# Two of every eight main P tiles moved into the remainder's transposing DMA, in the middle of the run too, with smaller rings for query, P and output

## The chip, the cores and the metric

The kernel runs on one core of one Trainium2 chip. The metric is the device time of one execution in microseconds (us). Three runs of the kernel before took 1221.61, 1224.74 and 1216.64 us, with a median of 1221.61.

## The reference

Two attention blocks, A and B, of the same shape are computed and their outputs set side by side. Each has its own x, K cache, V cache and weights, all bfloat16.

```python
B, Sq, D = 16, 144, 448
H, Sk, Dh = 16, 512, 256
q = (x @ wq).reshape(B, Sq, H, Dh).transpose(0, 2, 1, 3)
scores = einsum("bhqd,bhkd->bhqk", q, k_cache) * (Dh ** -0.5)
p = softmax(scores, axis=-1)
o = einsum("bhqk,bhkd->bhqd", p, v_cache)
out = o.transpose(0, 2, 1, 3).reshape(B, Sq, H * Dh) @ wo
```

The output is the concatenation of both blocks' `out` along the last axis.

## The kernel before

**Units and groups.** A unit is one (block, batch, head): 2 x 16 x 16 = 512 units. Eight units are a group (64 groups, called SG in the code); four are a half group (G). A head has 144 query rows, more than the 128 partitions. So the rows are split: 112 main rows ("A rows", QA) are treated unit by unit, and the 32 remaining rows ("B rows", QB) of four units are stacked into one 128-partition tile, so that a group has two B tiles.

**The work on a unit.** `t_q` (line 338) projects the query on TensorE into PSUM, and `t_evac_q` (lines 351, 355) brings it to `qt_sb`. `t_sa` (line 471) makes the scores of the A rows, `t_max` (482) takes the row maximum on VectorE, `t_exp` (493) the exponential on ScalarE into `pa_sb`, `t_recip` (503) and `t_norm` (511) normalise it, the latter on GpSimd (POOL in the profile). `t_ta` (524) transposes P on TensorE in four matmuls, and `t_evac_pta` (534) copies the result from PSUM to `pt_sb` on VectorE. `t_pv` (557) multiplies by V, `t_evac_ot` (572, 574) puts the result into the ring, and `t_op_piece` (595) does the output projection in pieces of two matmuls.

**The B rows.** `t_sb` (line 374) makes the scores of a whole group's B rows in 16 matmuls, followed by `t_max_b`, `t_exp_b` (397) and `t_norm_b` (415) into `pb_sb`. Their P reaches `pbt_sb` transposed in one of two ways. In the groups of `TB_SG` (0 to 7 and 28 to 37) TensorE does it (`t_tb`, line 437, four matmuls for each half group) and VectorE evacuates (447). In the other 46 groups one transposing DMA for the group does it (`t_ptb_dma`, line 425). `t_exp_b` writes its columns in the order that this DMA wants. From `pbt_sb`, which has one buffer, GpSimd copies each half group into `pt_sb` (`t_copy_ptb`, 457).

**Order.** All engines' programs are written out by one loop over slots `i`; a slot is the time of one unit's product with V (`t_pv(u)` at `i = u`). Group n's `t_sb` stands in slot 8n - lag, where the lag grows to 14 over the first groups (`LAGS`), and the eight `t_sa` of the group spread over the slots up to the next `t_sb`. TensorE runs its program strictly in this order. A B tile's copy to `pt_sb` stands in slots 8n - 1 and 8n + 1.

**Transfers.** All DMAs are issued by one queue, SyncE's (SP), in the order of `dma_plan`, which is sorted by planned slot; the `plan_*` functions hold each DMA's slot, its earliest slot and its deadline. Per group there are one K load of 2 MB (`t_load_k`, 306, a transposing DMA), two V loads of 1 MB (`t_load_v`, 316) and, outside `TB_SG`, the B rows' transposing DMA. Per four groups there is a load of x for two batches (`t_load_x`, 296 and 297, transposing too). K has two buffers (`NK`), so the K load of group n + 2 waits until the last `t_sa` of group n is done. From group 8 on the plan goes by pairs of groups:

```python
            plan_pb(t - 4, n)
            if n + 2 < NSG:
                plan_k(t - 3, n + 2)
            plan_pb(t + 2, n + 1)
            if n + 2 < NSG:
                plan_k(t + 2, n + 3)
            for j, at in enumerate((5, 5, 5, 8)):
                if 2 * n + 3 + j < NG:
                    plan_v(t + at, 2 * n + 3 + j)
```

The queue's order in a pair is thus: output stores and x (in every second pair), P of B rows, K of an even group, P of B rows, K of an odd group, four V. The weights of block B come in the middle of the run: `wq` in four blocks in slots 229 to 235 (lines 275, 277), `wo` around slots 277 and 293 (line 285).

Of the kernel before, what the change touches and what calls it, by code (L numbers as in the profile page):

```python
# [5 lines left out]
BF16 = mybir.dt.bfloat16  # L6
F32 = mybir.dt.float32
AF = mybir.ActivationFunctionType
ALU = mybir.AluOpType
# [3 lines left out]
PE, ACT, DVE, POOL, SP = "pe", "act", "dve", "pool", "sp"  # L13
# [109 lines left out]
def bass_concat_heads__mha_block_cached__gqa_block_cached__near_ridge_kernel(  # L123
# [20 lines left out]
    H, SK, DH = A_k_cache.shape[1], A_k_cache.shape[2], A_k_cache.shape[3]  # L144
    assert (SQ, D, SK, DH) == (144, 448, 512, 256), (SQ, D, SK, DH)
    assert H % 4 == 0
    QA, QB = 112, 32
    NU = Bn * H
    NT = NP * NU
    NG = NT // 4  # L150
    NSG = NT // 8
# [8 lines left out]
    NPC = NWO // OPP  # L160

    LT = 2
    LAGS = (7, 5, 6, 7, 8, 9, 10, 11, 12, 13, 14)
    RAMP = 8
    TB_SG = set(range(RAMP)) | set(range(NSG // 2 - 4, NSG // 2 + 6))
    NK, NV, NXG = 2, 5, 2
    WO_AT = ((12, 18, 26, 33), (277, 277, 293, 293))
    OP_FROM = (34, 34)
    N_WARM = (12, 16)
    XB = 2  # L170
    assert Bn % XB == 0
    NQT, NPA, NPB, NPT, NST, NSTB, NOST = 12, 14, 2, 8, 4, 2, 3
    NPBT = 1
    RS = 4
    RC = RS * 128
# [6 lines left out]
    with contextlib.ExitStack() as es:  # L182
        def sb(name, shape, dt):
            return es.enter_context(nc.sbuf_tensor(name, shape, dt))

        def ps(name, shape, dt):
            return es.enter_context(nc.psum_tensor(name, shape, dt))
# [6 lines left out]
        xt_sb = sb("xt_sb", [128, NXG, 4, XB * SQ], BF16)  # L194
        qt_sb = sb("qt_sb", [128, NQT, 2, SQ], BF16)
        pa_sb = sb("pa_sb", [128, NPA, SK], BF16)
        pb_sb = sb("pb_sb", [128, NPB, 2, SK], BF16)
        pt_sb = sb("pt_sb", [128, NPT, 4, SQ], BF16)
        pbt_sb = sb("pbt_sb", [128, NPBT, 2, 4, 128], BF16)
        ost_sb = sb("ost_sb", [128, NOST, D], BF16)  # L200
        ident = sb("ident", [128, 128], BF16)
        stat = sb("stat", [128, 3 * NST + 3 * NSTB + 2], F32)
        qp_ps = ps("qp_ps", [128, 512], F32)
        sa_ps = [ps("sa_ps%d" % i, [128, 512], F32) for i in range(2)]
# [6 lines left out]
        S = _Sched()  # L211
# [22 lines left out]
        NEG, RSUM, RINV = 0, NST, 2 * NST  # L234
# [3 lines left out]
        def t_ident():  # L238
            ones = pa_sb[:, 0, 0:128]

            def e1(g):
                return g.memset(ones, 1.0)
            S.add(POOL, e1, writes=[(("pa", 0), "ones")], name="ones")

            def e2(g):
                return g.affine_select(ident[:], ones, pattern=[[1, 128]], compare_op=ALU.is_equal,
                                       fill=0.0, base=0, channel_multiplier=-1)
            S.add(POOL, e2, reads=[(("pa", 0), "ones")], writes=[("ident", 0)], name="ident")

        def t_warm_zero():  # L250
            def e(v):
                return v.memset(pa_sb[:, 2:6, 0:128], 0.0)
            S.add(DVE, e, writes=[("warm", 0)], name="warmz")
# [166 lines left out]
        def t_ptb_dma(SG):  # L420
            psl = SG % NPB
            tsl = SG % NPBT

            def e(q):
                return q.dma_start_transpose(pbt_sb[:, tsl, :, :, :].rearrange("p g c q -> p (g c) q"),
                                             pb_sb[:, psl, :, :].rearrange("p g k -> p (g k)")).then_inc(
                    sems["pb%d" % tsl], 16)
            S.add(SP, e, reads=[(("pb", psl, g), (2 * SG + g, 1)) for g in range(2)],
                  writes=[(("pbt", tsl, g), SG) for g in range(2)], dma_sem="pb%d" % tsl, name="pb%d" % SG)

        def t_tb(G):
            psl = (G // 2) % NPB
# [19 lines left out]
        def t_copy_ptb(G):  # L452
            tsl = (G // 2) % NPBT
            s0 = (4 * G) % NPT

            def e(g):
                return g.tensor_copy(pt_sb[:, s0:s0 + 4, :, QA:SQ],
                                     pbt_sb[:, tsl, G % 2, :, :].rearrange("p c (j q) -> p j c q", j=4))
            S.add(POOL, e, reads=[(("pbt", tsl, G % 2), G // 2)], writes=[(("ptb", s0 + j), 4 * G + j) for j in range(4)],
                  name="cptb%d" % G)  # L460
# [16 lines left out]
        def t_max(U):  # L477
# [3 lines left out]
            def e(v):  # L481
# [2 lines left out]
            S.add(DVE, e, reads=[(("sap", bank), ("s", U))], writes=[(("neg", sl), U)], banks=["sa%d" % bank],  # L484
                  name="mx%d" % U)

        def t_exp(U):
            bank = U % 2
            sl = U % NST
            psl = U % NPA  # L490

            def e(a):
                return a.activation(pa_sb[0:QA, psl, :], sa_ps[bank][0:QA, :], AF.Exp,  # L493
                                    bias=stat[0:QA, NEG + sl:NEG + sl + 1], scale=1.0,
                                    accum_out=stat[0:QA, RSUM + sl:RSUM + sl + 1])
            S.add(ACT, e, reads=[(("sap", bank), ("s", U)), (("neg", sl), U)],
                  writes=[(("pa", psl), (U, 0)), (("rsum", sl), U)], banks=["sa%d" % bank], name="ex%d" % U)

        def t_recip(U):
            sl = U % NST  # L500
# [4 lines left out]

        def t_norm(U):
            sl = U % NST
            psl = U % NPA

            def e(g):  # L510
                return g.tensor_tensor(pa_sb[0:QA, psl, :], pa_sb[0:QA, psl, :],  # L511
                                       stat[0:QA, RINV + sl:RINV + sl + 1].to_broadcast([QA, SK]), op=ALU.mult)
            S.add(POOL, e, reads=[(("pa", psl), (U, 0)), (("rinv", sl), U)], writes=[(("pa", psl), (U, 1))],
                  name="nm%d" % U)

        def t_ta(U):
            psl = U % NPA
            bank = ta_bank[U]

            def e(t):  # L520
                src = pa_sb[0:QA, psl, :].rearrange("q (p c) -> q c p", c=4)
                ins = None
                for c in range(4):
                    ins = t.transpose(pta_ps[bank][:, c * 128:c * 128 + QA], src[:, c, :], ident[0:QA, 0:QA])  # L524
                return ins
            S.add(PE, e, reads=[(("pa", psl), (U, 1)), ("ident", 0)], writes=[(("sap", bank), ("t", U))],
                  banks=["sa%d" % bank], name="TA%d" % U)
# [101 lines left out]
        t_act_warm()  # L629
        t_wqzero()  # L630
        t_ident()
        t_warm_zero()
        ta_bank = {}
        lag = [LAGS[min(n, len(LAGS) - 1)] for n in range(NSG)]
        sb_slot = [8 * n - lag[n] for n in range(NSG)] + [8 * NSG - lag[-1]]
        sa_slot = [sb_slot[u // 8] + (u % 8) * (sb_slot[u // 8 + 1] - sb_slot[u // 8]) // 8 for u in range(NT)]
        q_slot = [sb_slot[0] - 1] * 8 + sa_slot[:NT - 8]
# [4 lines left out]
        tb_at = {}  # L642
        for n in TB_SG:
            t0 = 8 * n - 7
# [3 lines left out]
        s_min = sb_slot[0] - 4  # L648
        dma_plan = []

        def plan(at, lo, dl, fn, *args):
            assert lo <= at <= dl, (fn.__name__, args, lo, at, dl)
            dma_plan.append((at, len(dma_plan), fn, args))

        def plan_x(at, XG):
            n = XB * H
            plan(at, q_slot[(XG - 1) * n - 1] + 1 if XG >= NXG else s_min, q_slot[XG * n], t_load_x, XG)

        def plan_k(at, SG):
            plan(at, sa_slot[8 * (SG - NK) + 7] + 1 if SG >= NK else s_min, sb_slot[SG], t_load_k, SG)  # L660

        def plan_v(at, G):
            lo = 4 * (G - NV) + 3 + 1 if G >= NV else s_min
            plan(max(at, lo), lo, 4 * G, t_load_v, G)

        def plan_pb(at, SG):
            if SG not in TB_SG:
                plan(at, sb_slot[SG] + 5, 8 * SG - 1, t_ptb_dma, SG)
# [7 lines left out]
        for n in range(1, RAMP + 2):  # L676
            at = max(sb_slot[n] - 6, sa_slot[8 * (n - NK) + 7] + 1) if n >= NK else s_min + 2
# [10 lines left out]
        for n in range(RAMP, NSG, 2):  # L688
            t = 8 * n
            XG = (t + 32) // (XB * H)  # L690
            if (t + 32) % (XB * H) == 0 and XG < NXGT:
                plan_x(t - 4, XG)
            plan_pb(t - 4, n)
            if n + 2 < NSG:
                plan_k(t - 3, n + 2)
# [5 lines that stand above are left out]
                    plan_v(t + at, 2 * n + 3 + j)  # L701
        for hg in range(HG):
            lo = q_slot[NU - H + 4 * hg + 3] + 1
            plan((4.9, 4.9, 8, 11)[hg] + NU - 32, lo, q_slot[NU + 4 * hg], t_load_wq, 1, hg)
        dma_plan.sort(key=lambda t: t[:2])

        u_tail0 = NT - H
# [31 lines left out]
        i = s_min  # L739
        while True:  # L740
# [39 lines left out]
                t_copy_ptb((i + 1) // 4)  # L780
            if i % 8 == 1 and 0 <= i < NT:
                t_copy_ptb((i + 3) // 4)
            for u in sa_at.get(i - 1, ()):
                t_recip(u)
                t_norm(u)
            u = i + LT
            if 0 <= u < NT:
                ta_bank[u] = 1 - last_sa % 2 if sas else u % 2
                t_ta(u)
                t_evac_pta(u)  # L790
# [7 lines left out]
            u = i  # L798
            if 0 <= u < NT:
# [9 lines left out]
                if h == H - 1:  # L809
                    g_end = pr * RP + (b + 1) * SQ  # L810
                    lo = (pr * RP + b * SQ) // 128
# [80 lines left out]
```

## Time and profile before

| | |
|---|---|
| median of three runs | 1221.61 us |
| the profiled execution's own time | 1215.54 us |
| its span (first to last instruction) | 1213.8 us |
| mean granted TensorE clock | 0.992 |
| busy: TensorE matmuls / VectorE / ScalarE / GpSimd | 1171.0 / 743.7 / 748.6 / 727.9 us |
| chain that ended last | TensorE 80%, DMA 12%, VectorE 3%, GpSimd 2% |
| DMA | 679,424 packets, 304 MB on the queue of SP |
| the four P transposes of a unit on TensorE (line 524) | 2048 matmuls |
| their evacuation on VectorE (line 534) | 512 copies, 374 ns each |

The profile comes from one execution. Busy times of TensorE are unions of instructions whose ends are modelled, and matmuls overlap, so the time that a stage takes on TensorE is read from one stage's start to the next one's start. The landing of a DMA is the time of the last of its completions in the trace. "K of group n lands x us before `t_sb` of group n" is the slack of that load; where the slack is nearly nothing, TensorE waited for it.

### The profile page before, as it was taken

Reading aid. Unit: us, or ns where it says so; the run is one execution under the profiler, and the core shown is the slowest. Engines: PE = TensorE matmul, PEld = TensorE weight load, DVE = VectorE, ACT = ScalarE, POOL = GpSimd, SP = SyncE. Lnnn points to the kernel's source line nnn. Section 1 sums busy time; section 2 is a strip of 40 time slices with the busy share of each in tenths; the row PEclk is TensorE's granted clock in tenths of the full one; section 3 lists DMA queues with packets and bytes.
Section 4 is the critical chain, followed back from the end, with each engine's and each line's share of the span. In section 5 each row is a group of like instructions: output and inputs, shape, how many; then the busy total and the mean of one; then the engine's idle time right before and its main releaser. Section 6 shows DMA issues by size and latency. Waiting matters only on the chain.

```text
span 1213.8 us, 33200 instructions
## 1 busy us (share of the span) xinstructions
PE 1171.0 (96%) x13612; PEld 882.9 (73%) x13612; DVE 743.7 (61%) x2088; ACT 748.6 (62%) x2213; POOL 727.9 (60%) x774
## 2 busy tenths in 40 slices
PE   6898999999999999999899989999999999999989
PEld 3676777777777777777577767777777777777766
DVE  3676666656656666666566656666666566566661
ACT  2565666666656666666566656666666666566662
POOL 1675576666566666666465656666666665665661
PEclk9998999999999999999899999999999999999999
DMA  9999999999999999999999899999999999899971
GB/s 244 281 264 293 286 266 194 249 264 271 262 286 194 266 253 279 271 260 247 296 231 268 252 258 255 269 279 251 266 237 242 255 285 284 224 247 249 245 208 56
DMA packets 679577, 306.18 MB, mean 252 GB/s; under 512 B 597504, under 2 KB 610304, under 8 KB 679424
## 3 DMA queue, kind: packets, MB, share of 16 engines
q1 hardware_dynamic: 679424, 304.05, 104.6%
q8 instruction: 107, 1.75, 0.6%
q14 instruction: 46, 0.38, 0.1%
HBM read 148.90 MB, written 4.13 MB: 126 GB/s over the span
## 4 chain that ended last, share of the span: by engine, by line
PE 80%; DMA 12%; DVE 3%; POOL 2%; SPq 1%; issue 1%; ACT 1%; DVEq 0%
PE ot_ps L557 17%; PE qp_ps L338 17%; PE sa_ps L471 16%; PE op_ps L595 16%; PE sa_ps L524 7%; DMA kt_sb<-in_A_k_cache_dram 6%; DMA kt_sb<-in_B_k_cache_dram 6%; PE sb_ps L374 5%; POOL pa_sb L511 1%; DVE stat L482 1%; SPq L306 1%; POOL pb_sb L415 1%; PE sb_ps L437 1%; ACT pa_sb L493 1%; PE qp_ps L595 1%
## 5 line engine op out<-in xcount | busy, mean ns | idle before, releaser
L511 POOL TENSOR_TENSOR pa_sb<-pa_sb,stat 112x512 bf16<-112x512 bf16 x512 | 532.3, 1041 | 458.2 <-DVE stat L503 432.7
L493 ACT ACTIVATE pa_sb<-sa_ps,stat 112x512 bf16<-112x512 f32 x512 | 352.6, 689 | 405.8 <-DVE stat L482 403.6
L482 DVE TENSOR_REDUCE stat<-sa_ps 112x1 f32<-112x512 f32 x512 | 354.0, 691 | 335.3 <-PE sa_ps L471 330.7
L338 PEld LDWEIGHTS qp_ps<-xt_sb,wq_sb 128*128 128x128 bf16 x4048 | 284.1, 98 | 81.6 <-DMA wq_sb<-in_A_wq_dram 3.9
L557 PE MATMUL ot_ps<-pt_sb,v_sb 128*128 128x144 bf16 x4096 | 341.8, 226 | 0.0
L338 PE MATMUL qp_ps<-xt_sb,wq_sb 128*128 128x144 bf16 x4048 | 337.4, 227 | 4.6 <-DMA wq_sb<-in_A_wq_dram 4.2
L471 PE MATMUL sa_ps<-kt_sb,qt_sb 128*112 128x512 bf16 x1024 | 314.0, 388 | 6.0 <-DVE pt_sb L534 5.2
L595 PE MATMUL op_ps<-wo_sb,ring 128*128 128x448 bf16 x1120 | 275.1, 353 | 0.0
L557 PEld LDWEIGHTS ot_ps<-pt_sb,v_sb 128*128 128x128 bf16 x4096 | 269.5, 98 | 0.4
L524 PEld LDWEIGHTS sa_ps<-ident,pa_sb 112*128 112x128 bf16 x2048 | 159.9, 114 | 113.6 <-ACT pa_sb L493 38.3
L534 DVE COPY pt_sb<-sa_ps 128x448 bf16<-128x448 bf16 x512 | 191.4, 374 | 19.9 <-PE sa_ps L524 19.9
L572 ACT ACTIVATE ring<-ot_ps 128x288 bf16<-128x288 f32 (+8 forms) x512 | 191.0, 373 | 19.4 <-PE ot_ps L557 19.2
L524 PE MATMUL sa_ps<-ident,pa_sb 112*128 112x112 bf16 x2048 | 187.3, 213 | 6.1 <-ACT pa_sb L493 6.1
L351 DVE TENSOR_SCALAR qt_sb<-qp_ps 128x288 bf16<-128x288 f32 x252 | 115.2, 457 | 95.0 <-PE qp_ps L338 94.1
L415 POOL TENSOR_TENSOR pb_sb<-pb_sb,stat 128x512 bf16<-128x512 bf16 x128 | 133.3, 1041 | 0.0
L471 PEld LDWEIGHTS sa_ps<-kt_sb,qt_sb 128*112 128x112 bf16 x1024 | 96.8, 130 | 46.0 <-issue 28.4
L355 ACT ACTIVATE qt_sb<-qp_ps 128x288 bf16<-128x288 f32 x254 | 105.5, 415 | 33.2 <-PE qp_ps L338 31.6
L595 PEld LDWEIGHTS op_ps<-wo_sb,ring 128*128 128x128 bf16 x1120 | 96.0, 98 | 31.8 <-ACT ring L572 0.2
L493 ACT ACTIVATION_READ_ACCUMULATOR pa_sb<-sa_ps,stat 112x1 f32 x512 | 99.4, 194 | 0.0
L397 ACT ACTIVATE pb_sb<-sb_ps,stat 128x512 bf16<-128x512 f32 x128 | 88.6, 692 | 0.8
L387 DVE TENSOR_REDUCE stat<-sb_ps 128x1 f32<-128x512 f32 x128 | 87.2, 681 | 0.0
L374 PE MATMUL sb_ps<-kt_sb,qt_sb 128*32 128x512 bf16 x1024 | 69.2, 391 | 18.2 <-DMA kt_sb<-in_B_k_cache_dram 11.3
(33 smaller groups left out, 353.6 us busy)
## 6 DMA issues: line engine op xcount, KB each, us to landing
v_sb<-in_A_v_cache_dram SPq DMA_DIRECT2D x64, 1024.0 KB, 8.9
v_sb<-in_B_v_cache_dram SPq DMA_DIRECT2D x64, 1024.0 KB, 8.9
out_dram<-ost_sb SPq DMA_DIRECT2D x36, 112.0 KB, 9.7
wo_sb<-in_A_wo_dram SPq DMA_DIRECT2D x8, 448.0 KB, 9.5
wo_sb<-in_B_wo_dram SPq DMA_DIRECT2D x8, 448.0 KB, 5.2
wq_sb<-in_A_wq_dram SPq DMA_DIRECT2D x4, 768.0 KB, 6.0
wq_sb<-in_B_wq_dram SPq DMA_DIRECT2D x4, 768.0 KB, 9.7
pbt_sb<-pb_sb SPq DMA_TRANSPOSE x46, 4.9
```

The lines of the kernel that those rows point to most:

```text
L338: ins = t.matmul(acc[:, dc * SQ:(dc + 1) * SQ], lhsT=wq_sb[:, kc, c0:c0 + 128], rhs=xt_sb[:, xsl, kc, xo:xo + SQ], start=(kc == 0 and dc = ...
L374: ins = t.matmul(sb_ps[jj // 4][32 * j:32 * j + 32, :], lhsT=qt_sb[:, U % NQT, dc, QA:SQ], rhs=kt_sb[:, dc, (U % (8 * NK)) * SK:(U % (8 * ...
L415: return g.tensor_tensor(pb_sb[:, psl, G % 2, :], pb_sb[:, psl, G % 2, :], stat[:, RINVB + sl:RINVB + sl + 1].to_broadcast([128, SK]), op= ...
L471: ins = t.matmul(sa_ps[bank][0:QA, :], lhsT=qt_sb[:, U % NQT, dc, 0:QA], rhs=kt_sb[:, dc, ko:ko + SK], start=(dc == 0), stop=(dc == 1))
L482: return v.tensor_reduce(stat[0:QA, NEG + sl:NEG + sl + 1], sa_ps[bank][0:QA, :], axis=AX.X, op=ALU.max, negate=True)
L493: return a.activation(pa_sb[0:QA, psl, :], sa_ps[bank][0:QA, :], AF.Exp, bias=stat[0:QA, NEG + sl:NEG + sl + 1], scale=1.0, accum_out=stat ...
L511: return g.tensor_tensor(pa_sb[0:QA, psl, :], pa_sb[0:QA, psl, :], stat[0:QA, RINV + sl:RINV + sl + 1].to_broadcast([QA, SK]), op=ALU.mult)
L524: ins = t.transpose(pta_ps[bank][:, c * 128:c * 128 + QA], src[:, c, :], ident[0:QA, 0:QA])
L534: return v.tensor_copy(pt_sb[:, sl, :, 0:QA], pta_ps[bank][:, 0:512].rearrange("p (c q) -> p c q", c=4)[:, :, 0:QA])
L557: ins = t.matmul(ot_ps[ob][:, dc * SQ:(dc + 1) * SQ], lhsT=v_sb[:, vsl, j, c * DH + dc * 128:c * DH + (dc + 1) * 128], rhs=pt_sb[:, sl, c, ...
L572: ins = a.activation(ring[:, 2 * h:2 * h + 2, c0:c0 + n1], src[:, :, 0:n1], AF.Copy)
L595: ins = t.matmul(acc[0:m, 0:D], lhsT=ring[:, c, col0:col0 + m], rhs=wo_sb[:, c, :], start=(c == first), stop=(c == last))
```

## The change

Units 2 and 5 of every eight (`ADMA`), in every group but the first eight, write their normalised P into two further rows of `pb_sb` instead of `pa_sb`, with the column order of the B tiles. The group's transposing DMA takes four tiles instead of two. For these 112 units `t_ta` and `t_evac_pta` fall away, and GpSimd copies the transposed tile from `pbt_sb` to `pt_sb` (`t_copy_pta`), in slots 8n (unit 2) and 8n + 1 (unit 5). The middle groups 28 to 37 leave `TB_SG`, so their B rows go by DMA too. The lag grows over 12 groups instead of 11. The rings shrink to make room: query 12 to 9 slots, P 14 to 11, output 3 to 2. The load of x number 10 moves 16 slots ahead and the last block of `wq` of B five slots back. `pb_sb`'s unused partitions are set to zero once at the start.

```diff
-    LAGS = (7, 5, 6, 7, 8, 9, 10, 11, 12, 13, 14)
+    LAGS = (7, 5, 6, 7, 8, 9, 10, 11, 11, 12, 13, 14)
     RAMP = 8
-    TB_SG = set(range(RAMP)) | set(range(NSG // 2 - 4, NSG // 2 + 6))
+    TB_SG = set(range(RAMP))
+    ADMA = (2, 5)
+    NPX = 2 + len(ADMA)
...
-    NQT, NPA, NPB, NPT, NST, NSTB, NOST = 12, 14, 2, 8, 4, 2, 3
+    NQT, NPA, NPB, NPT, NST, NSTB, NOST = 9, 11, 2, 8, 4, 2, 2
...
-        pb_sb = sb("pb_sb", [128, NPB, 2, SK], BF16)
+        pb_sb = sb("pb_sb", [128, NPB, NPX, SK], BF16)
...
-        pbt_sb = sb("pbt_sb", [128, NPBT, 2, 4, 128], BF16)
+        pbt_sb = sb("pbt_sb", [128, NPBT, NPX, 4, 128], BF16)
...
+        def t_pb_zero():
+            def e(v):
+                return v.memset(pb_sb[96:128, :, 2:NPX, :], 0.0)
+            S.add(DVE, e, writes=[(("pb", psl, 2 + k), "z") for psl in range(NPB) for k in range(len(ADMA))], name="pbz")
...
-            S.add(SP, e, reads=[(("pb", psl, g), (2 * SG + g, 1)) for g in range(2)],
-                  writes=[(("pbt", tsl, g), SG) for g in range(2)], dma_sem="pb%d" % tsl, name="pb%d" % SG)
+            S.add(SP, e, reads=[(("pb", psl, g), (2 * SG + g, 1)) for g in range(2)] +
+                  [(("pb", psl, 2 + k), ("a", 8 * SG + j, 1)) for k, j in enumerate(ADMA)],
+                  writes=[(("pbt", tsl, g), SG) for g in range(NPX)], dma_sem="pb%d" % tsl, name="pb%d" % SG)
+
+        def by_dma(U):
+            return U % 8 in ADMA and U // 8 not in TB_SG
+
+        def t_copy_pta(U):
+            SG = U // 8
+            tsl = SG % NPBT
+            k = 2 + ADMA.index(U % 8)
+
+            def e(g):
+                return g.tensor_copy(pt_sb[:, U % NPT, :, 0:QA], pbt_sb[:, tsl, k, :, 0:QA])
+            S.add(POOL, e, reads=[(("pbt", tsl, k), SG)], writes=[(("pta", U % NPT), U)], name="cpta%d" % U)
...
             def e(a):
-                return a.activation(pa_sb[0:QA, psl, :], sa_ps[bank][0:QA, :], AF.Exp,
+                src = sa_ps[bank][0:QA, :]
+                if by_dma(U):
+                    src = src.rearrange("q (p c) -> q c p", c=4)
+                return a.activation(dst, src, AF.Exp,
...
-                plan_x(t - 4, XG)
+                plan_x(t - (20 if XG == 10 else 4), XG)
...
-            plan((4.9, 4.9, 8, 11)[hg] + NU - 32, lo, q_slot[NU + 4 * hg], t_load_wq, 1, hg)
+            plan((4.9, 4.9, 8, 16)[hg] + NU - 32, lo, q_slot[NU + 4 * hg], t_load_wq, 1, hg)
...
+            for k, j in enumerate(ADMA):
+                u = i + j - (1 if j > 2 else 0)
+                if (i - (1 if j > 2 else 0)) % 8 == 0 and 0 <= u < NT and by_dma(u):
+                    t_copy_pta(u)
...
-            if 0 <= u < NT:
+            if 0 <= u < NT and not by_dma(u):
                 ta_bank[u] = 1 - last_sa % 2 if sas else u % 2
                 t_ta(u)
                 t_evac_pta(u)
```

More of the change, by code (lines that the diff above doesn't have):

```diff
@@ L485, in t_max, with p_of @@
                   name="mx%d" % U)
+        def p_of(U):
+            if by_dma(U):
+                psl, k = (U // 8) % NPB, 2 + ADMA.index(U % 8)
+                return pb_sb[0:QA, psl, k, :], ("pb", psl, k), ("a", U)
+            psl = pa_slot[U]
+            return pa_sb[0:QA, psl, :], ("pa", psl), (U,)
         def t_exp(U):
@@ L489, in t_exp @@
             sl = U % NST
-            psl = U % NPA
+            dst, key, ver = p_of(U)
             def e(a):
-                return a.activation(pa_sb[0:QA, psl, :], sa_ps[bank][0:QA, :], AF.Exp,
+                src = sa_ps[bank][0:QA, :]
+                if by_dma(U):
+                    src = src.rearrange("q (p c) -> q c p", c=4)
+                return a.activation(dst, src, AF.Exp,
                                     bias=stat[0:QA, NEG + sl:NEG + sl + 1], scale=1.0,
@@ L496, in t_exp @@
             S.add(ACT, e, reads=[(("sap", bank), ("s", U)), (("neg", sl), U)],
-                  writes=[(("pa", psl), (U, 0)), (("rsum", sl), U)], banks=["sa%d" % bank], name="ex%d" % U)
+                  writes=[(key, ver + (0,)), (("rsum", sl), U)], banks=["sa%d" % bank], name="ex%d" % U)
         def t_recip(U):
@@ L507, in t_norm @@
             sl = U % NST
-            psl = U % NPA
+            dst, key, ver = p_of(U)
             def e(g):
[L511 to L514, printed above, removed]
+                return g.tensor_tensor(dst, dst, stat[0:QA, RINV + sl:RINV + sl + 1].to_broadcast([QA, SK]),
+                                       op=ALU.mult)
+            S.add(POOL, e, reads=[(key, ver + (0,)), (("rinv", sl), U)], writes=[(key, ver + (1,))], name="nm%d" % U)
         def t_ta(U):
-            psl = U % NPA
+            psl = pa_slot[U]
             bank = ta_bank[U]
@@ L632, in bass_concat_heads__mha_block_cached__gqa_block_cached__near_ridge_kernel @@
         t_warm_zero()
+        t_pb_zero()
         ta_bank = {}
+        pa_slot = {}
+        for u in range(NT):
+            if not by_dma(u):
+                pa_slot[u] = len(pa_slot) % NPA
         lag = [LAGS[min(n, len(LAGS) - 1)] for n in range(NSG)]
@@ L659, in plan_k @@
         def plan_k(at, SG):
-            plan(at, sa_slot[8 * (SG - NK) + 7] + 1 if SG >= NK else s_min, sb_slot[SG], t_load_k, SG)
+            lo = sa_slot[8 * (SG - NK) + 7] + 1 if SG >= NK else s_min
+            plan(max(at, lo), lo, sb_slot[SG], t_load_k, SG)
         def plan_v(at, G):
```

## The prediction

> **What bounds the kernel now.** I read the page first, then TensorE's instructions in order of time, then the DMA queue in order of time, then the waits.
>
> ```profile
> PE 1171.0 (96%) x13612; PEld 882.9 (73%) x13612; DVE 743.7 (61%) x2088; ACT 748.6 (62%) x2213; POOL 727.9 (60%) x774
> DMA  9999999999999999999999899999999999899971
> q1 hardware_dynamic: 679424, 304.05, 104.6%
> PE 80%; DMA 12%; DVE 3%; POOL 2%; SPq 1%; issue 1%; ACT 1%; DVEq 0%
> ```
>
> TensorE is busy for 96% of the span and VectorE, ScalarE and GpSimd for about 60%. But the DMA engines are full as well, and DMA holds 12% of the chain. The change takes work from TensorE and gives it to DMA, so the question is which of the two has less room. How much TensorE gains is read from starts, in one plain slot:
>
> ```profile
> 376.94 0.66 PE L338 MATMUL qp_ps<-xt_sb,wq_sb 128*128 128x144 bf16 x8
> 377.44 0.59 PE L471 MATMUL sa_ps<-kt_sb,qt_sb 128*112 128x512 bf16 x2
> 377.87 0.36 PE L524 MATMUL sa_ps<-ident,pa_sb 112*128 112x112 bf16 x4
> 378.07 0.67 PE L557 MATMUL ot_ps<-pt_sb,v_sb 128*128 128x144 bf16 x8
> ```
>
> The transposes (line 524) last 0.36 us on paper, but PV starts 0.20 us after them: a removed unit is worth 0.20 us. The other side is the queue of SP over two pairs of groups (start, duration of the issue):
>
> ```profile
> 378.52 1.23 SPq L425 DMA_TRANSPOSE pbt_sb<-pb_sb  x1
> 379.80 9.47 SPq L306 DMA_TRANSPOSE kt_sb<-in_A_k_cache_dram  x1
> 389.32 3.75 SPq L316 DMA_DIRECT2D v_sb<-in_A_v_cache_dram  x4
> 393.11 3.53 SPq L624 DMA_DIRECT2D out_dram<-ost_sb  x2
> 396.69 4.20 SPq L296 DMA_TRANSPOSE xt_sb<-in_A_x_dram  x1
> 400.92 1.26 SPq L297 DMA_TRANSPOSE xt_sb<-in_A_x_dram  x1
> 402.23 2.50 SPq L425 DMA_TRANSPOSE pbt_sb<-pb_sb  x1
> 404.77 8.39 SPq L306 DMA_TRANSPOSE kt_sb<-in_A_k_cache_dram  x1
> ```
>
> The landings of these, from the trace's completions: P 382.72, K of group 21 392.03, fourth V 404.15, x 405.87, P 408.29, K of group 22 415.23. The scores of group 22's remainder begin at 415.56: a slack of 0.33 us. Over the run the even K loads are the tight ones: 0.0 to 0.9 us of slack where an x lies in the pair, 1.8 to 5.3 us where none does, and odd ones 5 to 8 us. So TensorE sets the pace, but in every second pair DMA is level with it. Where K is late, it shows as this:
>
> ```profile
> PE sb_ps L374 <- DMA kt_sb<-in_B_k_cache_dram: 11.3, 5, 5.3
> PE sb_ps L374 <- DMA kt_sb<-in_A_k_cache_dram: 6.5, 4, 3.2
> ```
>
> **The change on TensorE.** 112 units lose their transposes: 112 x 0.20 = 22.4 us. The middle's ten groups lose two sets of four (line 437, 0.226 us from start to start): 20 x 0.226 = 4.5 us. A group without waits takes 17.96 us between starts of line 374; it becomes 17.56, a pair 35.1. VectorE loses 112 x 0.374 us and 20 x 0.416 us, which is worth nothing with 39% idle.
>
> **The change on DMA.** Alone in the queue, transposed packets of 256 bytes run at one rate, shown by a window inside a K load (TensorE, loads, VectorE, ScalarE, GpSimd, clock, DMA share, GB/s):
>
> ```profile
> 408.00:412.00 4.00, 4.00 (x47) 3.08 (x45) 2.56 (x8) 2.16 (x6) 3.15 (x4) 1.00 1.27 290
> ```
>
> A remainder's DMA is 0.26 MB, 0.91 us at this rate; behind an output store it adds a median of 0.87 us to the queue, so the rate holds for it. Doubled, it adds 0.91 us. 46 go from 1024 to 2048 packets and ten are new: 67,584 packets, 60 us of transfer. The trace has 80 us before 1185 in which no packet is under way, in pieces behind K's buffer wait and the issue latency. The 60 us would fit if the holes lay where they are needed; they lie in the pairs that have slack already. The extra cost of one doubled DMA is bounded by nothing (the issue lasts 1.2 us for line 297's smaller x as well, so issue may not grow) and 2.33 us, the median added by one that finds the queue running dry. I take 0.91, the row of a full queue, because the queue is full there.
>
> A page of the Trainium skill gives another price. "DMA: Bandwidth & Descriptors", section "Where 436 GB/s comes from", says that transposes from SBUF to SBUF are bound by the fabric at 435 GB/s rather than by HBM. By that estimate the doubled part would cost 0.60 us; the trace's 0.87 us for the same bytes speaks against it, and by the page the steady sum below would be some 6 us smaller.
>
> **GpSimd.** It gains 112 copies. Line 457 copies 128x512 in 0.611 us; 448 columns are 0.53, together 60 us on 728. It isn't the bound. But the one `pbt_sb` buffer is free only after its last copy, and that is now unit 5's, behind the second half group's (377.88 to 378.49 in the trace; the P DMA starts at 378.52). So the DMA of the next group, and the K load queued behind it on SP, start 0.53 us later (bounds 0.53 and 0.61).
>
> **A round of four groups.** Before: groups 20 to 24 take 451.63 - 379.54 = 72.1 us. After, counted from the scores of group 20:
> - Pair with x: K of 22 landed at 35.69. Add the copy 0.53 and two doubled DMAs 1.82: 38.04. TensorE is there at 36.02 - 0.80 = 35.2 and waits 2.8 us. The nine such pairs of the trace lie within 0.9 us early and 1.4 us late, 0.1 late on average.
> - Pair without x, after a wait: the next P DMA is queued behind the late K, and no hole is left. From K to K this took 32.45, 31.56 and 31.70 us in the trace where a wait came before; plus 1.82 it is 33.4 to 34.3, under 35.2. TensorE is in time.
>
> Together 38.0 + 35.2 = 73.2, 1.1 us more than before. There are 10.5 such rounds (groups 10 to 28 and 38 to 62): **+12 us**. What TensorE saves is given back as waits for K in every second pair, with the extra transfer on top.
>
> **The middle.** Here the ten groups had no such DMAs. K of 28 to K of 32 took 601.12 - 522.20 = 78.9 us, bound by DMA at the end (TensorE idle for 5.3 us). Now one doubled DMA (0.91) and three new ones (1.81 each) come in, and the last `wq` block (some 2.5 us) moves behind K of 32: +3.8; TensorE starts that stretch without its former slack, so about +4. From 32 to 38 it took 112.6 us, of which some 10 us were holes (two gaps of 3.2 and 4.0 us with nothing outstanding, and two first-packet latencies of 1.9). Six new DMAs are 10.9 us and the `wq` block 2.5; moving x 10 changes only the order within: +3 at least, +4 with a small hole left. **+8 us.** With all ten at 2.33 us more it would be +15; with the holes used twice as well, 0.
>
> **The clock.** Waits have an aftermath:
>
> ```profile
> 714.00:718.00 4.00, 4.00 (x33) 2.32 (x26) 1.54 (x4) 0.82 (x3) 0.70 (x1) 0.57 1.27 286
> ```
>
> After idles of 3.20, 3.38 and 5.28 us the granted clock fell to a half for 6.8, 3.4 and 6.8 us; after those of 1.75 us or less in mid-run it didn't. Waits of 2.8 us lie just under. A late P tile also delays its copy and so PV two slots before the scores, which splits the wait. I take two falls in the long run and one more in the middle, 1.7 us each, less slack: **+4 us**; bounds 0 and 10 falls, 17 us.
>
> The Trainium skill ("TensorE: Matmul & The Clock Gate", section "HAM oscillation — how this bites in real kernels") warns that DMA waits beyond a window of about 3.4 us restart the array cold each time. The trace's idle of 3.20 us did so too, and by the page's bare figure none of the 2.8 us waits would.
>
> **At nothing.** Nine query slots: unit u + 8 takes the slot of u - 1, whose scores lie one slot back on TensorE. Eleven P slots serve six units of eight, as 14 did for eight. Two output slots: chunks come 13 to 14 slots apart, a store waits at most 15 and lands within 12 us; if that cover went, ScalarE would wait in `t_evac_op`. The strided exponential is like line 397, 692 against 689 ns. The zeroing is under 1 us at the start, while `wq` loads. The slower lag leaves the first 180 us as they are: no packet-free time is left there, DMA decides. Groups 8, 9, 62 and 63 save 1.6 us in all.
>
> **Sum.** 1213.8 + 12 + 8 + 4 - 1.6 = 1236 us of span, 1238 with the 1.7 us around it. The three runs' median is 6 us above the profiled execution; with a third of that, 1240.
>
> **Rivals.**
> - **DMA packs, TensorE stays the bound (faster).** The 60 us go into the 80 us of holes. For it: the holes are 16.6 of the 220 us from 180 to 400, so a round's transfers are 66.7 us, with four doubled DMAs' 3.6 us 70.3, no more than TensorE's 70.2. Then 1215.5 - 27 and some 7 us of waits: 1182; but DMA needs 1104 busy us + 60 + 4 before and 24 behind = 1192 of span. So 1194 to 1209. Against it: K's two buffers forbid running ahead.
> - **A draw.** Half the surcharge is absorbed: rounds of 72.2, the middle +4: 1212 to 1232.
> - **Collapse into the slow clock.** If each wait with x passes 3 us, ten falls at 1.7 to 3.4 us on top: 1258 to 1272. It decides from 0.4 us more per pair.
> - **GpSimd becomes the bound** by waiting in order for late P: 788 busy us of 1215 and 11 P slots of lead speak against; it would look like the collapse.
> - **The change doesn't do what it says**, if PV waits for the copies in slots 8n and 8n + 1: P lands some 4 us before the late scores, so at most inside the same wait; no time of its own.
>
> **How the numbers follow.** Forecast (1232 to 1258) 0.52, collapse 0.08, draw 0.26, faster 0.14. A measurement tells about 1% from no change: 1209 and 1234 around 1221.6. Faster takes the first rival but for its edge, 0.13; the draw and the forecast's lowest part give 0.29; slower 0.58. The range leaves out the rival below 1212 and the collapse above 1260. The forecast's own range is 1232 to 1258.
>
> **What would show it.** Right: waits of line 374 on K growing from 18 to over 40 us, every second even K 2 to 4 us late, odd K in time; line 524 with 1600 matmuls; packet-free time well under 80 us; groups 28 to 38 near 198 us instead of 190. Wrong: rounds under 71 us, or TensorE waiting for anything else than K.

## The result, and the profile after

The changed kernel takes 1261.1 us (median of 4 runs, 1252.6 to 1261.9) against 1219.1 us: 1.034 times the time before, with a 95% interval of 1.032 to 1.037. I had forecast slower, 1240 us, with 1232 to 1258 as the forecast's own range and 1260 as the outer bound; the measured time lies just above both. The direction holds, but the loss of 42 us is more than twice the 18 that I worked out. The page of the changed kernel (busy times, DMA slices, the queue of SP, the chain by engine):

```profile
PE 1163.9 (92%) x13084; PEld 861.8 (68%) x13084; DVE 705.7 (56%) x1957; ACT 746.5 (59%) x2213; POOL 781.6 (62%) x886
DMA  9999999999999999999999999999999999999992
q1 hardware_dynamic: 747328, 321.36, 109.9%
PE 66%; DMA 23%; DVE 3%; ACT 3%; SPq 1%; issue 1%; POOL 1%; DVEq 0%
```

TensorE has 528 matmuls fewer and 4% less of the span; DMA moved 17 MB more and its part of the chain went from 12% to 23%. The difference between the two packet counts is 67,904, the 67,584 that I had counted and 320 more. GpSimd went from 728 to 782 us and stayed far from the bound. The waits of TensorE for K (line 374 before is 381 now; total, times, longest):

```profile
PE sb_ps L381 <- DMA kt_sb<-in_B_k_cache_dram: 30.5, 12, 5.1
PE sb_ps L381 <- DMA kt_sb<-in_A_k_cache_dram: 24.6, 12, 3.9
```

From 17.8 us in 9 waits they grew to 55.1 us in 24. The queue of SP over the same two pairs as in the prediction (start, duration of the issue):

```profile
403.56 4.78 SPq L303 DMA_TRANSPOSE xt_sb<-in_A_x_dram  x1
408.38 1.26 SPq L304 DMA_TRANSPOSE xt_sb<-in_A_x_dram  x1
409.69 4.10 SPq L432 DMA_TRANSPOSE pbt_sb<-pb_sb  x1
413.83 8.65 SPq L313 DMA_TRANSPOSE kt_sb<-in_A_k_cache_dram  x1
422.53 3.13 SPq L432 DMA_TRANSPOSE pbt_sb<-pb_sb  x1
425.70 8.37 SPq L313 DMA_TRANSPOSE kt_sb<-in_A_k_cache_dram  x1
```

x landed at 414.1, P at 417.2, K of group 22 at 425.92; the scores of group 22 began at 425.97. P added 3.1 us to the queue behind x, against 2.4 before.

Where the time went, by stretches between the remainder's scores of two groups (from the profiled executions, one of each kernel; the last column is the sum of the waits for K as above):

| kernel | median us | 10 to 28 | 28 to 38 | 38 to 62 | waits |
|---|---|---|---|---|---|
| before | 1219.1 | 324.1 | 190.3 | 435.6 | 17.8 |
| after | 1261.1 | 339.3 | 202.6 | 454.9 | 55.1 |
| matmuls ahead of the waits (e1) | 1256.9 | 337.1 | 203.7 | 451.2 | 21.0 |
| doubled DMA alone (e2) | 1249.2 | 339.5 | 191.3 | 452.2 | 43.8 |
| TensorE's saving alone (e3) | 1215.6 | 323.8 | 190.3 | 434.9 | 26.4 |
| e3, no transposing DMA of P (e11) | 1194.0 | 316.3 | 184.4 | 427.3 | 16.3 |

### The profile page after: what moved, and what is told of

Its sections match the earlier page's. It is cut to its first block, busy times and chain, and to the rows that moved or that the text cites. A ratio compares the mean times of both kernels' runs of the same rounds, so it can differ in the third digit from the quotient of the medians.

```text
span 1260.2 us, 32092 instructions
## 1 busy us (share of the span) xinstructions
PE 1163.9 (92%) x13084; PEld 861.8 (68%) x13084; DVE 705.7 (56%) x1957; ACT 746.5 (59%) x2213; POOL 781.6 (62%) x886
## 4 chain that ended last, share of the span: by engine, by line
PE 66%; DMA 23%; DVE 3%; ACT 3%; SPq 1%; issue 1%; POOL 1%; DVEq 0%
PE ot_ps L586 14%; PE qp_ps L345 14%; PE sa_ps L491 14%; PE op_ps L624 13%; DMA kt_sb<-in_A_k_cache_dram 11%; DMA kt_sb<-in_B_k_cache_dram 11%; PE sb_ps L381 5%; PE sa_ps L553 5%; DVE stat L502 2%; ACT pa_sb L523 1%; SPq L313 1%; POOL pa_sb L541 1%; DVE qt_sb L358 1%; ACT ost_sb L642 1%; PE qp_ps L624 0%
## 5 line engine op out<-in xcount | busy, mean ns | idle before, releaser
L541 POOL TENSOR_TENSOR pa_sb<-pa_sb,stat 112x512 bf16<-112x512 bf16 x400 | 416.0, 1042 | 363.0 <-DVE stat L533 263.9
L523 ACT ACTIVATE pa_sb<-sa_ps,stat 112x512 bf16<-112x512 f32 x400 | 275.2, 688 | 363.9 <-DVE stat L502 362.9
L586 PE MATMUL ot_ps<-pt_sb,v_sb 128*128 128x144 bf16 x4096 | 346.4, 228 | 12.7 <-issue 11.8
L586 PEld LDWEIGHTS ot_ps<-pt_sb,v_sb 128*128 128x128 bf16 x4096 | 278.6, 99 | 36.9 <-issue 12.9
L553 PEld LDWEIGHTS sa_ps<-ident,pa_sb 112*128 112x128 bf16 x1600 | 123.2, 115 | 102.0 <-ACT pa_sb L523 51.1
L563 DVE COPY pt_sb<-sa_ps 128x448 bf16<-128x448 bf16 x400 | 149.0, 373 | 21.6 <-PE sa_ps L553 21.6
L541 POOL TENSOR_TENSOR pb_sb<-pb_sb,stat 112x512 bf16<-112x512 bf16 x112 | 116.6, 1041 | 70.0 <-DVE stat L533 69.9
L553 PE MATMUL sa_ps<-ident,pa_sb 112*128 112x112 bf16 x1600 | 148.7, 216 | 9.1 <-ACT pa_sb L523 9.1
L362 ACT ACTIVATE qt_sb<-qp_ps 128x288 bf16<-128x288 f32 x254 | 105.3, 415 | 35.8 <-PE qp_ps L345 35.2
L381 PE MATMUL sb_ps<-kt_sb,qt_sb 128*32 128x512 bf16 x1024 | 73.6, 411 | 55.1 <-DMA kt_sb<-in_B_k_cache_dram 30.5
L523 ACT ACTIVATE pb_sb<-sa_ps,stat 112x512 bf16<-112x512 f32 x112 | 77.0, 688 | 76.8 <-DVE stat L502 76.7
L477 POOL COPY pt_sb<-pbt_sb 128x512 bf16<-128x512 bf16 x128 | 78.3, 612 | 29.7 <-DMA pbt_sb<-pb_sb 19.7
## 6 DMA issues: line engine op xcount, KB each, us to landing
out_dram<-ost_sb SPq DMA_DIRECT2D x36, 112.0 KB, 10.4
```

Source lines behind the costliest of these rows:

```text
L381: ins = t.matmul(sb_ps[jj // 4][32 * j:32 * j + 32, :], lhsT=qt_sb[:, U % NQT, dc, QA:SQ], rhs=kt_sb[:, dc, (U % (8 * NK)) * SK:(U % (8 * ...
L523: return a.activation(dst, src, AF.Exp, bias=stat[0:QA, NEG + sl:NEG + sl + 1], scale=1.0, accum_out=stat[0:QA, RSUM + sl:RSUM + sl + 1])
L541: return g.tensor_tensor(dst, dst, stat[0:QA, RINV + sl:RINV + sl + 1].to_broadcast([QA, SK]), op=ALU.mult)
L563: return v.tensor_copy(pt_sb[:, sl, :, 0:QA], pta_ps[bank][:, 0:512].rearrange("p (c q) -> p c q", c=4)[:, :, 0:QA])
L586: ins = t.matmul(ot_ps[ob][:, dc * SQ:(dc + 1) * SQ], lhsT=v_sb[:, vsl, j, c * DH + dc * 128:c * DH + (dc + 1) * 128], rhs=pt_sb[:, sl, c, ...
```

## Experiments

The theory after the first reading was that the transfers alone set the pace of every pair of groups, with or without x. The rivals were the clock (falls to half speed after the waits), GpSimd's copies out of the one `pbt_sb` buffer, and the smaller rings.

**e1: fill the waits.** The changed kernel with 32 matmuls ahead of every even group's scores, from 12 on.

```diff
                 if u % 8 == 0:
+                    if u // 8 >= 12 and u // 8 % 2 == 0:
+                        t_fill(u // 8)
                     t_sb(u // 8)
...
+        def t_fill(SG):
...
+                for _ in range(32):
+                    ins = t.matmul(sb_ps[1][:, 0:128], lhsT=ident[:, :], rhs=ident[:, :], start=True, stop=True)
```

> The changed kernel with 32 further matmuls of 128 columns (some 1.8 us) on TensorE ahead of the remainder's scores of every even group from 12 on, in place of part of the wait for K. DMA theory (the transfers alone set the pace of every pair): K lands when it did, so 1258 to 1265 us. Clock theory (the falls to half speed after waits of 2 to 5 us cost much of the 42 us): waits shrink under 2 us, the falls vanish, 1235 to 1250 us. If the extra matmuls lie on the path, 1275 us or more.

1256.9 us, 1.030 of before (1.025 to 1.035), between the two bands and just under the DMA theory's. The clock rose to 0.992 from 0.974, as the slices of the two pages show (after first, then this run):

```profile
PEclk9998999999999899999899989999999998999999
```
```profile
PEclk9999999999999999999899989999999999999999
```

After group 10 there are three falls to a half instead of twelve, none of them in the two long stretches, and the run is only 4 us shorter, within the intervals of both ratios. These 4 us are net of what the matmuls cost: in 13 of the 26 places the scores began 0.25 to 1.9 us later than they could have without them, 13.9 us in all. So I estimate that the nine falls were worth at most 18 of the 42 us. As the main cause the clock falls; its exact part isn't shown. In the other 13 places the matmuls cost nothing, which says again that TensorE was waiting there.

**e2: the doubled DMA without anything else.** The kernel before with two tiles of zeros added to the transposing DMA of its 46 groups. Its smaller rings and its buffers aren't shown here; e4 tries the rings alone.

```diff
-                return q.dma_start_transpose(pbt_sb[:, tsl, :, :, :].rearrange("p g c q -> p (g c) q"),
-                                             pb_sb[:, psl, :, :].rearrange("p g k -> p (g k)")).then_inc(
+                return q.dma_start_transpose(pbt_sb[:, :, :, :].rearrange("p g c q -> p (g c) q"),
+                                             pb_sb[:, 2 * psl:2 * psl + 4, :].rearrange("p g k -> p (g k)")).then_inc(
```

> The kernel before with the remainder's transposing DMA doubled by two tiles of zeros that nobody reads, in its 46 groups; TensorE's work as before, rings of 9 query, 13 P and 2 out slots, no further copies on GpSimd. DMA theory: an even P transfer costs 1.5 us more, every pair with x gets a wait of 2 to 3 us, 1235 to 1250 us. GpSimd theory (the further copies out of the one buffer hold the queue up): no copies, so 1217 to 1225 us.

1249.2 us, 1.022 (1.018 to 1.027). Outside the middle this one edit costs 15.4 and 16.6 us, nearly as much as the whole change does (15.2 and 19.3). No copy on GpSimd was added, so the buffer theory falls too.

**e3: TensorE's saving without the doubling.** The changed kernel, with two tiles in the DMA.

```diff
-                return q.dma_start_transpose(pbt_sb[:, tsl, :, :, :].rearrange("p g c q -> p (g c) q"),
-                                             pb_sb[:, psl, :, :].rearrange("p g k -> p (g k)")).then_inc(
+                return q.dma_start_transpose(pbt_sb[:, tsl, 0:2, :, :].rearrange("p g c q -> p (g c) q"),
+                                             pb_sb[:, psl, 0:2, :].rearrange("p g k -> p (g k)")).then_inc(
...
-                return g.tensor_copy(pt_sb[:, U % NPT, :, 0:QA], pbt_sb[:, tsl, k, :, 0:QA])
+                return g.tensor_copy(pt_sb[:, U % NPT, :, 0:QA], pbt_sb[:, tsl, k - 2, :, 0:QA])
```

> The changed kernel, but the transposing DMA moves only the two tiles of the remainder; the copies of units 2 and 5 read the remainder's tiles in place of their own, so the transposed P of these units is left out of the computation. TensorE's saving, the copies, the rings and the plan stay. DMA theory: the saving of 27 us comes through, less what the middle's ten new DMAs of normal size cost, 1192 to 1212 us. GpSimd or ring theory: still 1235 us or more.

1215.6 us, 0.998 (0.995 to 1.000). This misses the DMA theory's 1192 to 1212, on the side that I had not thought of: 27 us less work on TensorE yield 3 us. (The edits of the plan, worth 6 us by themselves in e5, and the middle's ten new DMAs of two tiles are in this figure too.) All idle of TensorE in pieces of over 0.15 us grows from 37.9 to 57.0 us, the waits for K among it from 17.8 to 26.4:

```profile
PE sb_ps L381 <- DMA kt_sb<-in_B_k_cache_dram: 14.3, 8, 4.2
PE sb_ps L381 <- DMA kt_sb<-in_A_k_cache_dram: 12.1, 9, 3.0
```

**e4: the rings alone.**

```diff
-    NQT, NPA, NPB, NPT, NST, NSTB, NOST = 12, 14, 2, 8, 4, 2, 3
+    NQT, NPA, NPB, NPT, NST, NSTB, NOST = 9, 13, 2, 8, 4, 2, 2
```

> The kernel before with 9 query slots, 13 P slots and 2 out slots (11 P slots would not hold all eight units of its lead). Ring theory (a slot that isn't free yet holds TensorE or ScalarE): 1230 us or more. DMA, clock and GpSimd theories: 1215 to 1224 us, as before.

1221.6 us, 1.001 (0.999 to 1.003): nothing. The change's own 11 P slots are in e3, which is no slower than before.

**e5: the edits of the plan alone**, on the kernel before (the lag over 12 groups, x 10 and the last `wq` block moved; with them, as in the change, no K load is planned ahead of its earliest slot).

> The kernel before with the change's three edits of the plan alone: x 10 ahead by 16 slots, the last block of the second wq five slots later, the lag over 12 groups. If the middle's two long waits for K (5.3 and 3.4 us, with a slow clock after them) come from the order of those loads, they shrink and the run takes 1208 to 1215 us; if the transfers of the middle alone set its length, 1216 to 1221 us as before.

1212.9 us, 0.995 (0.992 to 0.998). The middle shrinks from 190.3 to 186.5 us. This beats the kernel before by half a per cent and the changed one by 4.

**e7: one unit in the DMA.** `ADMA = (5,)` and 13 P slots.

> The changed kernel with unit 5 alone in the transposing DMA (three tiles instead of four, 13 P slots). DMA theory with a price in proportion to the packets: about half of the loss, 1236 to 1244 us. If a DMA of more than two tiles no longer fits ahead in the queue and SP is held up whatever its size: 1250 us or more. If TensorE's saving counts as soon as the queue has some room: 1225 us or less.

1229.8 us, 1.010 (1.005 to 1.016), between the third band and the first. With two, three and four tiles in the DMA the time is 1215.6, 1229.8 and 1261.1 us: 14 us for the third tile and 31 for the fourth, so less than in proportion at first (unit 2's saving on TensorE is missing here, which e3 shows to be worth little). A row of the queue shows the same: behind an output store, where no instruction fetch falls into it, the P transfer adds a median of 0.85 us with two tiles (13 transfers, e3), 1.31 with three (11, e7) and 2.38 with four (8, the changed kernel). The third tile costs 0.46 us and the fourth 1.07.

**e8: the bytes without the transposing.** The kernel before with a plain copy beside each of its 46 DMAs.

```diff
+                return q.dma_start(pc_sb[:, :], pz_sb[:, :]).then_inc(sems["pb%d" % tsl], 16)
```

> The kernel before with a plain copy of two tiles of zeros (0.26 MB, nobody reads it) issued behind each of the 46 transposing DMAs of the remainder: the bytes of the doubling without its transposed packets. If the bytes at their plain rate are the price (0.67 us each, against 1.5 us for the doubling that took 1249 us): 1228 to 1236 us. If any further DMA between two K loads costs a fixed time: 1243 us or more. If only transposed packets of 256 bytes are dear: 1218 to 1226 us.

1239.3 us, 1.017 (1.012 to 1.021), between the first two bands. The plain copies cost two thirds of what the transposed packets do, more than their plain rate gives. That isn't the price of the bytes alone, because 46 further DMAs are issued here, and in e10 as many further transposing issues cost 12 us. Most of the loss lies in the first stretch (339.8 us against 324.1 before; the last has 442.5 against 435.6); why, stays open.

**e9: the clock once more, on e3.** `t_fill` as in e1, at groups 14, 18 and so on.

> The run with two tiles in the DMA and TensorE's saving kept (1215.6 us), with 32 further matmuls of 128 columns ahead of the remainder's scores of every fourth group (14, 18, ...), where TensorE waits for K behind x. Clock theory: the saving was lost in falls of the clock, so 1202 to 1210 us. DMA theory: pairs with x last as long as their transfers whatever TensorE does, so 1211 to 1220 us.

1221.6 us, 1.003 (1.000 to 1.006): no gain, and just beyond the upper band. The saving wasn't lost in the clock: in its two long stretches e3 is at half speed for 11.8 us, which can hide 6 us at most.

**e10: the doubling in two DMAs.** As e2, but four tiles go as two DMAs of two.

> The kernel before with the doubling of zeros as in the run that took 1249.2 us, issued as two transposing DMAs of two tiles each instead of one of four. If one DMA of four tiles is dear because it doesn't fit ahead in the queue and holds SP up: two small ones cost little more than twice 0.9 us, 1230 to 1240 us. If the transposed packets themselves are the price, in whatever DMAs: 1246 to 1256 us.

1261.2 us, 1.036 (1.032 to 1.040), above both bands. Cutting the DMA in two doesn't help, and the 46 further issues add 12 us to e2. It doesn't rule out that SP is held up: behind an output store, the K load that follows P is issued 0.2 us before the store lands in e2 and here alike (medians of 11), against 3.6 us in the kernel before.

**e11: no transposing DMA of P at all.** As e3, with 32 KB of plain copy in its place.

```diff
-                return q.dma_start_transpose(pbt_sb[:, tsl, 0:2, :, :].rearrange("p g c q -> p (g c) q"),
-                                             pb_sb[:, psl, 0:2, :].rearrange("p g k -> p (g k)")).then_inc(
+                return q.dma_start(pbt_sb[:, tsl, 0, 0, :], pb_sb[:, psl, 0, 0:128]).then_inc(
```

> The changed kernel, but a plain copy of 32 KB stands in for every transposing DMA of P; the transposed P of the remainder (from group 8 on) and of units 2 and 5 is left out of the computation. TensorE's saving, the copies on GpSimd, the rings and the plan stay. DMA theory: with some 1 us less per group on the queue TensorE is the bound again and its saving of 27 us shows, 1186 to 1203 us. If something else than DMA kept the saving back at two tiles (1215.6 us): 1210 us or more.

1194.0 us, 0.980 (0.977 to 0.983), 22 us under e3 by 51,072 packets less on the queue. Once DMA has room, TensorE's saving appears: the two long stretches are 7.8 and 8.3 us shorter than before, where 0.40 us a group makes 7.2 and 9.6. (There is also less P on the queue than before the change, so this isn't the saving alone.) The chain is TensorE's again:

```profile
PE 79%; DMA 9%; DVE 4%; ACT 4%; SPq 1%; issue 1%; POOL 1%; DVEq 0%
```

**e12: the other way round.** e5 with the remainder of groups 12, 16, 20 and so on, whose DMA follows x, on TensorE.

> The kernel before with the three edits of the plan (1212.9 us), and with the remainder of groups 12, 16, 20 and so on, whose DMA stands behind x in the queue, transposed on TensorE as in the middle. DMA theory: each pair with x loses 1.4 us on the queue and TensorE gets 0.45 us more; the waits there were 0 to 1.4 us, so about even, 1207 to 1216 us. If TensorE alone sets the pace: 1217 to 1222 us, for 10 groups' transposes.

1214.7 us, 0.995 (0.993 to 0.998), the same as e5. Outside the middle these are nine groups, not ten. TensorE waits less for K (12.6 us against 19.3 in e5) and works more: the kernel before stands where work can be moved between the two without gain.

## Why the prediction was half right

**The mechanism held in the two long stretches.** The waits sit where I put them, at line 381 on K of even groups, after a longer P transfer in a full queue; the odd loads are in time (2.9 us of slack and more). Line 553 has 1600 matmuls. The rings, the strided exponential, the zeroing and the slower lag cost nothing, as priced (e4 and e3; e5 for the lag with the rest of the plan). One sign of being wrong came true in the middle, where TensorE waited for P as well (below).

**The step that failed is the round of four groups.** I had +1.1 us for 10.5 rounds, 12 us. The stretches show (15.2 + 19.3) / 10.5 = 3.3 us per round, 34.5 us together (the clock's falls, for which I had 3.4 us more in these stretches, are in this). The two pairs, from K to K landing, mean over the pairs without `wq` or `wo` loads outside the middle:

| pair | before | forecast | after | e1 | e3 |
|---|---|---|---|---|---|
| with x | 38.6 | 38.0 (from the scores) | 39.6 | 37.7 | 38.6 |
| without x | 33.8 | 33.4 to 34.3 | 36.5 | 37.1 | 34.2 |

The pair without x is the larger miss: from scores to scores, as my sum counts, the two take 38.8 and 36.9 us after, where I had 38.0 and 35.2. I took as its base the three fastest pairs of the trace (31.6 to 32.5 us), though two more that follow a wait took 35.1 and 34.0, and put TensorE's 35.2 above them; from K to K it takes 36.5, so TensorE waits in both kinds of pair (21 even loads have less than 0.2 us of slack, 9 before).

**The size of one doubled DMA** is the term of that sum that was mis-sized. I priced the doubling at 0.91 us by the rate of a K load, supported by the 0.87 us that a P transfer adds behind an output store. Where no instruction fetch falls into it, such a transfer adds a median of 2.38 us after and 0.86 before (8 transfers each): the doubling costs 1.5. The rate of the short one held for the third tile, as e7 shows, and not for the fourth.

Two things in the traces go with this. First, a P transfer that runs alone is slower than a K load. Behind a store this shows less, because some of its packets go while the store is still landing (before, the first of them end 2.2 us ahead of the store's landing, by the median). The window of a P transfer running alone in the trace after, and of a K load (TensorE, loads, VectorE, ScalarE, GpSimd, clock, DMA share, GB/s):

```profile
465.00:467.00 2.00, 2.00 (x27) 1.62 (x24) 1.32 (x4) 0.59 (x2) 0.47 (x1) 1.00 1.16 215
471.00:474.00 3.00, 3.00 (x36) 2.45 (x35) 1.55 (x5) 1.56 (x5) 1.42 (x2) 1.00 1.29 294
```

215 against 294 GB/s. From the 100th to the 900th packet of such a transfer, 1.20 ns pass per packet, against 0.89 for K. By this rate I estimate 81 us for the 67,584 new packets, not 60. Second, SP is held up. Behind a store, the K load that follows P is issued 3.6 us before the store lands in the kernel before, 2.1 with three tiles (e7) and 0.2 with four (medians), and it lands 9.6, 10.4 and 11.6 us after the store. No run here separates the two. The time without any packet before 1185 fell from 80.5 to 28.8 us: some 50 us went into holes and the rest made the run longer. The bound of 2.33 us that I kept for the range held this price; I put the middle of the range on the wrong row.

The Trainium skill ("DMA: Bandwidth & Descriptors", section "Where 436 GB/s comes from") has transposes from SBUF to SBUF bound by the fabric side, at 435 GB/s. Here one that ran alone moved 215 GB/s, less than the 294 of a transpose from HBM, and the measurement decides.

**The middle** took 12.3 us more, where I had 8. With normal-size DMAs (e3) it takes 190.3 us, as before, of which the moved loads give 3.8 (e5); so the ten new transfers cost about 4 and their doubling 12, 1.2 us each. Part of it isn't a wait for K. I had said that a late P tile costs no time of its own; here PV (line 586 now) waited twice, 7.21 and 4.59 us, until P had landed and GpSimd had copied it. The total, and the first of the two with its copy (start, duration):

```profile
PE ot_ps L586 <- issue: 11.8, 2, 7.2
612.98 0.61 POOL L477 COPY pt_sb<-pbt_sb 128x512 bf16<-128x512 bf16 x1 [7.92 <-DMA pbt_sb<-pb_sb]
613.69 1.12 PE L586 MATMUL ot_ps<-pt_sb,v_sb 128*128 128x144 bf16 x8 [7.21 <-issue]
```

This P transfer was issued at 600.09, behind V, `wq` and an output store, and landed at 612.92. It is the longest wait of TensorE in the run.

**The clock** was priced at 4 us for three falls in all. There were twelve after group 10. What they were worth stays open: e1 leaves between 4 and, by estimate, 18 us. I had also misread a row: the idle of 1.75 us that I took for harmless lies at 23 us and was followed by 3.4 us at half speed; the longest harmless one in mid-run was 1.17 us.

**TensorE's saving** I had counted into the pairs without x, where TensorE was to be the bound. e3 shows that it was worth 0.3 and 0.7 us in the two long stretches, with pairs from K to K as long as before (table), and e11 that it appears when the queue is relieved: the queue was the second bound already. TensorE's saved work came back as 19 us more of idle, 8.6 of them waits for K.

**Among the rivals**, "DMA packs" came nowhere near: the holes did fill, but the packets cost a third more than in its sum, by the estimate above. The collapse into the slow clock has the right time, 1258 to 1272, and its falls came; but e1, which takes nine of the twelve out, is only 4 us faster, so that this time was hit by luck.

**Left open:** how the 2.2 us of the round that I missed divide between the packet rate, the late issue of K, the instruction fetches and the clock, and why the first stretch of e8 lost most.

## What to carry to other kernels

When two resources are both over 90% busy, price a move between them on the receiver at its average load, not by the stretches in which it ran best, and test the giver's saving alone: here it was worth 3 of 27 us. Price a transfer by a row of its own kind and of its own size: here the short one's 0.87 us behind a store held for half as much again and not for twice as much. And idle time of a queue counts only where the program's order lets the new work start.

## What the hardware showed

**Instruction fetches hold transposing transfers up.** The trace's second DMA queue fetches instructions in pieces of 16 KB, about one in 11 us. The last 7,000 packets of a K load take a median of 6.39 us where no fetch ends among them (35 loads of the kernel before) and 7.69 us where one does (29 loads). The changed kernel has 6.38 and 7.71 us. One such hole, in the trace after, behind a fetch at 448.2 us:

```profile
450.00:451.00 1.00, 1.00 (x12) 0.71 (x11) 0.91 (x2) 0.67 (x2) 0.01 (x1) 1.00 0.04 5
```

5 GB/s for a microsecond in which a P transfer was under way. More time in transposing transfers means more of these hits; that part, and that the fetch is the cause, is read from traces and not tried by itself.

**The clock falls after shorter waits than I had seen.** Idles of 2.10, 2.26, 2.30 and 2.60 us were followed by 3.4 us at half speed; those of 2.22 and 2.75 us weren't. What tells them apart is a grid: all steps of the clock in the 13 traces lie a multiple of 3.413 us apart. Between 100 and 1185 us, each of the 64 falls from full to half speed follows a stretch of this grid in which TensorE was idle for 1.95 us or more in sum; of the other 3,967 stretches at full speed none has more than 1.94. The idles of 2.22 and 2.75 us were cut by the grid and left 1.28 and 1.85 us in one stretch. The Trainium skill ("TensorE: Matmul & The Clock Gate", section "HAM oscillation — how this bites in real kernels") sets the limit at about 3.4 us of idle. Here it is lower.

**A transposing issue ends late.** In the kernel before, SP's issue of a K load takes 9.4 us of the 12.1 us until the load lands (medians), and in all runs it ends 1.9 to 5.1 us before the landing. So what stands behind a K load on SP starts when the load is nearly done.
